# V and U by feature held pair by pair, and float64 weights rounded by one integer addition in pieces of 384 columns

## The chip, the cores and the metric

The kernel runs on one core of one Trainium2 chip. The metric is the device time of one execution in microseconds (us), as the median of the runs shown. A core has five engines that work side by side, each through its own list of instructions in a fixed order: TensorE (PE in the profile, with its weight loads shown as PEld), VectorE (DVE), ScalarE (ACT), GpSimd (POOL) and SyncE (SP), which here does nothing but start transfers. An engine waits when an operand is not ready, and everything behind the waiting instruction on that engine waits with it.

## The reference

A recurrent attention runs over 768 tokens for 4 batches of 8 heads of 40 features (32 pairs of batch and head), and two feed-forward blocks follow on the 3072 tokens of 320 features:

```python
for t in range(S):                                    # S = 768
    y[:, :, t] = einsum('bhd,bhde->bhe', r_t, state)
    Sa = einsum('bhde,bhe->bhd', state, a_t)
    state = state * w_t[:, :, None, :] - einsum('bhd,bhe->bhde', Sa, b_t)
    state = state + einsum('bhd,bhe->bhde', v_t, k_t)
x = y by token                                        # (3072, 320)
x = square(maximum(x @ w_in, 0)) @ w_out              # 320 -> 2048 -> 320
out = ((x @ w_a) * (x @ w_b)) @ w_out2                # 320 -> 1536 -> 320
```

The weight matrices of both blocks are float64 (the inputs are drawn times a float64 scalar), so their 8-byte values reach the chip as pairs of 32-bit words. The kernel makes float32 of them itself.

## The kernel before

**Attention.** The tokens are cut into 24 waves of 32 tokens. Each wave is worked as matrices: `prep1` and `prep2` form products of a, k, b and w alone, every four waves `inv_ops` inverts a triangular matrix in 31 steps on DVE and POOL, and then the wave's own chain runs: `m_z` (PE, then a copy on ACT), `m_s` (copies on ACT), `m_ut` (PE, then the ACT copies at L291 into `VUT`), `m_r` (PE, then ACT copies `VU` and DVE masks `RVR`), `m_st` (PE, then DVE adds the state `VS`) and `m_y` (PE, then DVE scales `Y`, and SP stores it). `VUT` holds V (first 32 of 64 places, loaded by SP at L260) and U (last 32, written by ACT at L291) by feature, for 16 pairs; `m_r` uses the 64 columns of one pair as the weights of a matmul, 32 matmuls a wave, each of which the trace shows as two PE instructions. `prep2` does the same arithmetic with `KBT` in place of `VUT`, and `KBT` is laid out as 16 pairs of 64 columns side by side.

**Weights.** `Weights.load` turns float64 into float32 in pieces: SP loads `raw` (L392), ACT squares the high words (L397), DVE drops tiny values (L398), ACT converts the low words (L401), DVE builds the result and its scale in three instructions (L407, L410, L413), POOL multiplies and adds (L414, L415). For the first block `put` then splits the value into a rounded high part (ACT, L440) and the rest (POOL, L433), and the parts go to DRAM (`w1s`) except for a few blocks of 128 columns of w_in that stay in SBUF (`RESIDENT`). The second block's float32 values go to `w2s`.

**Streams.** From wave 4 on, the first block's matmuls (L430, `Stream`) are put between the matmuls of the waves, at places that `emit` counts out by a rate; blocks that are not resident are loaded from `w1s` again for each of the six groups of 512 tokens (L607), into two buffers. A piece of weights is decoded whenever the matmuls issued add up to a share of `TICK_NS`. After the last wave come the rest of the first block and the whole second block.

**Order.** PE's order is the order of the code from wave 4 on, and a scheduler's before. The other engines' orders come from the same scheduler, and on the chip they are fixed. Every transfer is started by SP, in order.

Of the kernel before, what the change touches and what calls it, by code (L numbers as in the profile page):

```python
# [9 lines left out]
F32 = mybir.dt.float32  # L10
# [7 lines left out]
D = 40  # L18
NP = 16
TW = 32  # L20
GW = 4
TOK = 512

DW = 192
PARTS = ((0, 6), (6, 11), (11, 16))
# [25 lines left out]

LEAST_HIGH = 1.125 * 2.0**-15

# [5 lines left out]
class Attention:  # L59
# [8 lines left out]
    def __init__(s, tc, sb, ps, wakb, rv, vt, xs, n_waves):  # L68
# [3 lines left out]
        def t(name, shape):  # L72
            return sb.tile(shape, F32, name=name)
# [11 lines left out]
        s.Z = t("Z", [128, 320])  # L85
        s.VUT = t("VUT", [104, 64, NP])
        s.VU = t("VU", [128, 640])
# [192 lines left out]
    def m_ut(s, w):  # L280
        inv = s.InvT[:, w % GW]
        for h in range(2):
# [6 lines left out]
            for e in range(2):  # L289
                r = slice(64 * e, 64 * e + D)  # L290
                s.nc.scalar.copy(out=s.VUT[r, 32:64, 8 * h:8 * h + 8].rearrange("p t a -> p a t"), in_=pv[r])  # L291

    def m_r(s, w, part):
# [5 lines left out]
        for p in range(p0, p1):  # L299
            o = slice(80 * (p - p0), 80 * (p - p0) + 80)  # L300
            s.mm(85, ps[64:128, o], s.VUT[0:40, :, p], s.eye_and(s.RVR, slice(0, 40), 0, p))
            s.mm(85, ps[0:64, o], s.VUT[64:104, :, p], s.eye_and(s.RVR, slice(64, 104), 1, p))
        pv = cols(ps[:, 0:80 * n], 80)
# [65 lines left out]
class Weights:  # L369
# [19 lines left out]
    def load(s, src, n, put):  # L389
        nc = s.nc  # L390
        raw = s.sb.tile([128, DW, 2], I32, tag="raw", name="raw", bufs=4)
        nc.sync.dma_start(out=raw[:, 0:n].rearrange("p n k -> p (n k)"), in_=src.bitcast(I32))  # L392

        def first():
            low, high = raw[:, 0:n, 0], raw[:, 0:n, 1].bitcast(F32)
            y = s.sb.tile([128, DW], F32, tag="dy", name="dy", bufs=4)[:, 0:n]
# [5 lines left out]
            return lambda: second(y, low.bitcast(F32))  # L402

        def second(y, low):
            z = s.sb.tile([128, DW], F32, tag="dz", name="dz")[:, 0:n]
            yi, zi = y.bitcast(I32), z.bitcast(I32)
            nc.vector.tensor_scalar(  # L407
                out=zi, in0=yi, scalar1=0x07FFFFFF, scalar2=3, op0=ALU.bitwise_and, op1=ALU.logical_shift_left
            )
            nc.vector.scalar_tensor_tensor(  # L410
                out=yi, in0=yi, scalar=-0x40000000, in1=zi, op0=ALU.bitwise_and, op1=ALU.bitwise_or
            )
            nc.vector.tensor_scalar(out=zi, in0=yi, scalar1=-0x00800000, scalar2=None, op0=ALU.bitwise_and)  # L413
            nc.gpsimd.tensor_tensor(out=low, in0=low, in1=z, op=ALU.mult)  # L414
            s.engine.tensor_tensor(out=y, in0=low, in1=y, op=ALU.add)  # L415
            return lambda: put(y)

        return first


class Moe:
# [13 lines left out]
    def add_w1(s, weights, src, wa, wb, done):  # L435
# [11 lines left out]
        def last(x):  # L447
            put(x, wb[:, 160:320], wb[:, 544:640], wb[:, 320:384])
            done()

        for o in (0, 192):
            weights.add(src[:, o:o + 192], 192, lambda x, o=o: put(x, wa[:, o:o + 192], wa[:, 384 + o:576 + o]))
        weights.add(src[:, 384:544], 160, lambda x: put(x, wb[:, 0:160], wb[:, 384:544]))
        weights.add(src[:, 544:704], 160, last)

# [352 lines left out]
def attention_moe(ctx, tc, wakb, rv, vt, wm1, wm2, nat, out):  # L808
# [367 lines left out]
```

## Time and profile before

| | |
|---|---|
| median of 3 runs | 1364.19 us (1359.73 to 1364.43) |
| profiled execution | 1365.23 us, of which its span 1363.5 us |
| PE busy | 1189.4 us (87% of the span) |
| DVE busy | 836.8 us (61%) |
| ACT busy | 559.5 us (41%) |
| POOL busy | 468.6 us (34%) |

The span is that of one profiled execution, and 1.7 us of its time lie outside it. Shares of busy time are means over stages that differ much, so stretches of the span are read apart: up to about 88 us the first preparations and the first inversion, to 217 us the waves 0 to 3 without a stream, to 890 us the waves 4 to 23 with the stream between them, to 958 us the rest of the first block, and then the second block alone. PEclk is the share of TensorE's full clock that was granted; it has two levels, 1.00 and 0.50 (2.4 and 1.2 GHz), and a figure between them is a mean over both.

### The profile page before, as it was taken

What the parts mean: (1) busy time and instruction counts of PE and PEld (TensorE: products, weight loads), DVE (VectorE), ACT (ScalarE), POOL (GpSimd) and SP (SyncE); (2) the same over time, 40 slices, a digit from 0 to 9 for tenths busy, and PEclk for the clock granted to TensorE, in tenths of its full rate; (3) what the DMA queues carried; (4) which work ended last, traced back from release to release, by engine and by line L of the source; (5) the groups of instructions that cost most, each with busy time, mean ns of one, the idle gap of its engine ahead of it and who ended that gap; (6) DMA issues with size and microseconds to landing.
All of it is one profiled execution on the core that took longest, in us unless ns stands there. A gap on an engine that the chain in (4) does not pass through costs nothing.

```text
span 1363.5 us, 35301 instructions
## 1 busy us (share of the span) xinstructions
PE 1189.4 (87%) x14178; PEld 966.2 (71%) x14178; DVE 836.8 (61%) x1831; ACT 559.5 (41%) x1289; POOL 468.6 (34%) x738
## 2 busy tenths in 40 slices
PE   2536644799889998999899999999998999999997
PEld 2535543676667776777677777778886888888886
DVE  6988898878987898789877733353331332332222
ACT  2224434474455545554554453565221222222221
POOL 3567774755243534453444100000798000000000
PEclk9995555899999999999899999999999999999999
DMA  6225536454366536554563333483221000000000
GB/s 176 52 67 162 157 110 186 124 151 138 109 184 176 160 109 184 161 169 117 172 174 96 106 109 90 160 280 120 75 74 42 12 32 16 20 16 20 14 7 22
DMA packets 87652, 148.28 MB, mean 109 GB/s; under 512 B 11560, under 2 KB 54056, under 8 KB 85416
## 3 DMA queue, kind: packets, MB, share of 16 engines
q1 hardware_dynamic: 87480, 145.94, 36.4%
q8 instruction: 114, 1.87, 0.6%
q14 instruction: 58, 0.48, 0.1%
HBM read 117.06 MB, written 25.69 MB: 105 GB/s over the span
## 4 chain that ended last, share of the span: by engine, by line
PE 46%; POOL 7%; DMA 3%; DVE 3%; issue 1%; ACT 1%; SPq 1%; POOLq 0%; DVEq 0%; ACTq 0%
PE h L430 15%; PE b L430 8%; PE x L430 8%; PE a L104 8%; PE o L430 7%; POOL w_t L683 3%; POOL w_ok L684 3%; DMA raw<-wm 1%; DMA x2s<-xl 1%; DMA w<-w1s 0%; DMA inp<-wakb 0%; DVE tmp L236 0%; DMA xl<-xs 0%; DVE Ball L243 0%; DVE VS L323 0%
## 5 line engine op out<-in xcount | busy, mean ns | idle before, releaser
L430 PE MATMUL h<-xhl,w 128*128 128x512 f32 x768 | 233.7, 425 | 7.0 <-DMA w<-w1s 5.9
L561 DVE TENSOR_TENSOR b<-b,a 128x512 f32<-128x512 f32 x72 | 50.4, 699 | 213.4 <-PE b L430 199.3
L430 PEld LDWEIGHTS h<-xhl,w 128*128 128x128 f32 x768 | 142.2, 196 | 41.2 <-DMA w<-w1s 6.2
L430 PE MATMUL x<-gh,w 128*128 128x512 f32 x480 | 147.7, 420 | 5.0 <-DMA w<-w1s 3.4
L414 POOL TENSOR_TENSOR raw<-raw,dz 128x192 f32<-128x192 f32 (+2 forms) x136 | 82.3, 605 | 164.9 <-DVE dz L413 39.2
L430 PE MATMUL h<-xhl,w2h 128*128 128x512 f32 x360 | 128.0, 396 | 0.0
L104 PEld LDWEIGHTS a<-RVR,VUT 40*64 40x64 f32 x1536 | 96.5, 204 | 41.1 <-issue 20.0
L104 PE MATMUL a<-KA,KBT 40*64 40x80 f32 x1536 | 85.5, 269 | 45.1 <-POOL KBT L182 21.8
L104 PE MATMUL a<-RVR,VUT 40*64 40x80 f32 x1536 | 107.9, 290 | 18.6 <-ACT VUT L291 4.9
L430 PE MATMUL b<-xhl,w2h 128*128 128x512 f32 x360 | 120.9, 401 | 0.0
L104 PEld LDWEIGHTS a<-KA,KBT 40*64 40x64 f32 x1536 | 74.5, 164 | 62.6 <-POOL KBT L182 35.8
L433 DVE TENSOR_TENSOR gl<-h,gh 128x512 fp32r<-128x512 f32 x96 | 66.1, 689 | 84.1 <-ACT h L499 80.4
L563 ACT CAST gh<-b 128x512 fp32r<-128x512 f32 x72 | 42.3, 587 | 163.8 <-DVE b L561 163.8
L430 PEld LDWEIGHTS x<-gh,w 128*128 128x128 f32 x480 | 89.0, 194 | 27.3 <-ACT raw L401 4.1
L497 ACT ACTIVATE h<-h 128x512 f32<-128x512 f32 x96 | 55.9, 582 | 98.5 <-PE h L430 95.6
L430 PE MATMUL x<-gl,w 128*128 128x512 f32 x288 | 95.8, 427 | 0.0
L558 ACT COPY a<-h 128x512 f32<-128x512 f32 x72 | 42.3, 587 | 121.2 <-PE h L430 121.1
L415 POOL TENSOR_TENSOR dy<-raw,dy 128x192 f32<-128x192 f32 (+2 forms) x136 | 88.7, 652 | 8.5
L430 PE MATMUL b<-xhl,w2l 128*128 128x512 f32 x216 | 86.1, 399 | 0.0
L430 PE MATMUL h<-xhl,w2l 128*128 128x512 f32 x216 | 85.9, 397 | 0.0
L430 PE MATMUL o<-w2h,gl 128*128 128x320 f32 x288 | 85.6, 309 | 0.0
L430 PE MATMUL o<-w2l,gh 128*128 128x320 f32 x288 | 85.5, 308 | 0.0
(97 smaller groups left out, 2387.8 us busy)
## 6 DMA issues: line engine op xcount, KB each, us to landing
w<-w1s SPq DMA_DIRECT2D x60, 384.0 KB
w<-w1s SPq DMA_DIRECT2D x60, 320.0 KB
raw<-wm SPq DMA_DIRECT2D x92, 192.0 KB
inp<-wakb SPq DMA_DIRECT2D x48, 322.7 KB
w2f<-w2s SPq DMA_DIRECT2D x12, 544.0 KB
w2s<-dy SPq DMA_DIRECT2D x60, 96.0 KB
raw<-wm SPq DMA_DIRECT2D x32, 160.0 KB
VS<-vt SPq DMA_DIRECT2D x48, 80.0 KB
```

What stands on the lines that cost most here:

```text
L104: s.nc.tensor.matmul(out, lhsT=lhsT, rhs=rhs, start=True, stop=True)
L414: nc.gpsimd.tensor_tensor(out=low, in0=low, in1=z, op=ALU.mult)
L415: s.engine.tensor_tensor(out=y, in0=low, in1=y, op=ALU.add)
L430: s.nc.tensor.matmul(out, lhsT=lhsT, rhs=rhs, start=start, stop=stop)
L433: (engine or s.nc.vector).tensor_tensor(out=out, in0=x, in1=hi.bitcast(F32), op=ALU.subtract)
L497: s.nc.scalar.activation(out=ps, in_=ps, func=ACTF.Relu)
L558: s.nc.scalar.copy(out=a, in_=pa)
L561: s.nc.vector.tensor_tensor(out=pb, in0=pb, in1=a, op=ALU.mult)
L563: s.nc.scalar.copy(out=ch, in_=pb)
L683: nc.gpsimd.tensor_scalar(out=t, in0=x, scalar1=lim, scalar2=None, op0=op)
L684: nc.gpsimd.tensor_tensor(out=s.ok, in0=s.ok, in1=t, op=ALU.mult)
```

## The change

`VUT` becomes `[104, 16, 64]`: a pair's 64 columns lie side by side, as they do in `KBT`. The host no longer exchanges tokens and pairs in v, so that SP's load of V goes to 16 places of 32 tokens (128 bytes) in each row, where it was one run of 512 tokens (2 KB).

A piece of weights has up to 384 columns instead of 192, so that there are 68 pieces instead of 136. In each, DVE takes the sign, ACT converts the low word to a float between 2 and 4 (whose bits count from the exponent's lowest place), ACT takes the absolute value of the high word, DVE raises it to a least value, DVE shifts it left by three bits and puts the sign in, and one 32-bit integer addition on POOL adds the low word's bits, which rounds: two instructions on ACT, three on DVE and one on POOL, where there were two, four and two. `raw` and `dy` have three buffers instead of four, five blocks stay resident instead of six, and the prologue has two `KBT` buffers instead of three.

```diff
-DW = 192
+DW = 384
-PIECES = 8
+PIECES = 4
-DECODE = {0: 28, 1: 28, 2: 28, 3: 28}
-RESIDENT = (2, 4, 7, 9, 12, 14)
+DECODE = {0: 14, 1: 14, 2: 14, 3: 14}
+RESIDENT = (2, 5, 8, 11, 14)
-DEC0 = 6
+DEC0 = 3
...
-        s.VUT = t("VUT", [104, 64, NP])
+        s.VUT = t("VUT", [104, NP, 64])
...
-                out=s.VUT[64 * e:64 * e + D, 0:32], in_=cols(s.rv[w, e, :, 1], NP)
+                out=s.VUT[64 * e:64 * e + D, :, 0:32], in_=cols(s.rv[w, e, :, 1], TW)
...
-                s.nc.scalar.copy(out=s.VUT[r, 32:64, 8 * h:8 * h + 8].rearrange("p t a -> p a t"), in_=pv[r])
+                s.nc.scalar.copy(out=s.VUT[r, 8 * h:8 * h + 8, 32:64], in_=pv[r])
...
-            s.mm(85, ps[64:128, o], s.VUT[0:40, :, p], s.eye_and(s.RVR, slice(0, 40), 0, p))
+            s.mm(85, ps[64:128, o], s.VUT[0:40, p], s.eye_and(s.RVR, slice(0, 40), 0, p))
...
-        raw = s.sb.tile([128, DW, 2], I32, tag="raw", name="raw", bufs=4)
+        raw = s.sb.tile([128, DW, 2], I32, tag="raw", name="raw", bufs=3)
...
-            s.pin(nc.scalar.activation(out=y, in_=high, func=ACTF.Square))
-            s.pin(nc.vector.scalar_tensor_tensor(
-                out=y, in0=y, scalar=LEAST_HIGH**2, in1=high, op0=ALU.is_ge, op1=ALU.mult
...
-            s.pin(nc.scalar.activation(out=low.bitcast(F32), in_=low.bitcast(U32), func=ACTF.Copy, scale=2.0**-52))
...
+            s.pin(nc.vector.tensor_scalar(out=yi, in0=high, scalar1=-0x80000000, scalar2=None, op0=ALU.bitwise_and))
+            s.pin(nc.scalar.activation(
+                out=low.bitcast(F32), in_=low.bitcast(U32), func=ACTF.Copy, bias=2.0, scale=2.0**-51
...
+            s.pin(nc.scalar.activation(out=size, in_=high.bitcast(F32), func=ACTF.Abs))
...
+            nc.vector.tensor_scalar(out=size, in0=size, scalar1=TINY_HIGH, scalar2=None, op0=ALU.max)
+            nc.vector.scalar_tensor_tensor(
+                out=yi, in0=size.bitcast(I32), scalar=3, in1=yi, op0=ALU.logical_shift_left, op1=ALU.bitwise_xor
             )
...
-            nc.vector.tensor_scalar(out=zi, in0=yi, scalar1=-0x00800000, scalar2=None, op0=ALU.bitwise_and)
-            nc.gpsimd.tensor_tensor(out=low, in0=low, in1=z, op=ALU.mult)
-            s.engine.tensor_tensor(out=y, in0=low, in1=y, op=ALU.add)
+            nc.gpsimd.tensor_tensor(out=yi, in0=yi, in1=low, op=ALU.add)
...
-        kbts = [at.KBT] + [pre.tile([104, NP, 64], F32, name=f"KBT{i}") for i in range(1, 3)]
+        kbts = [at.KBT] + [pre.tile([104, NP, 64], F32, name=f"KBT{i}") for i in range(1, 2)]
```

PE's 3026 rows stand in the same order in both programs. On the other engines the scheduler's order moves with the pieces. Counted on ACT, 37 of 136 pieces are begun ahead of wave 4's copy of `Z` before, and 25 of 68 now; ahead of wave 10's it is 88 and 41. Of the 16 blocks, the ten that move need the first 40 pieces before, and the eleven that move need the first 22 now.

On DVE, in wave 1, the rows from the first mask of `RVR` to its last were these before the change:

```order
L307 TENSOR_TENSOR RVR<-a,mask 64x192 x2
L407 TENSOR_SCALAR dz<-dy 128x192
L410 SCALAR_TENSOR_TENSOR dy<-dy,dz 128x192
L413 TENSOR_SCALAR dz<-dy 128x192
L398 SCALAR_TENSOR_TENSOR dy<-dy,raw 128x192
L307 TENSOR_TENSOR RVR<-a,mask 64x160 x2
L407 TENSOR_SCALAR dz<-dy 128x192
L410 SCALAR_TENSOR_TENSOR dy<-dy,dz 128x192
L413 TENSOR_SCALAR dz<-dy 128x192
L307 TENSOR_TENSOR RVR<-a,mask 64x160 x2
```

On DVE, at the same place, they are these now (line numbers are one higher, and L412, L413 and L402 are the new decode):

```order
L308 TENSOR_TENSOR RVR<-a,mask 64x192 x2
L308 TENSOR_TENSOR RVR<-a,mask 64x160 x2
L412 TENSOR_SCALAR dz<-dz 128x320
L413 SCALAR_TENSOR_TENSOR dy<-dz,dy 128x320
L402 TENSOR_SCALAR dy<-raw 128x384
L308 TENSOR_TENSOR RVR<-a,mask 64x160 x2
```

Seven instructions on 192 columns between the masks have become three on 320 or 384.

On SP, where the stream's first weights are fetched back, the rows from the load of wave 4's tokens to the first loads of `w` were these before (`w1s` with its block's number is the stored weights, `xhl` and `xl` the tokens of the first group):

```order
L460 DMA xhl<-xs_57 128x2x512
L462 DMA xl<-xs_57 64x512 x2
L392 DMA raw<-wm 128x320
L257 DMA VS_147<-vt 32x640
L860 DMA w1s_640_87<-w_1750 128x640
L257 DMA VS_147<-vt 32x640
L392 DMA raw<-wm 128x384
L607 DMA w_2148<-w1s_768_70 128x768
L392 DMA raw<-wm 128x384
L860 DMA w1s_768_88<-w_1878 128x768
L607 DMA w_2152<-w1s_768_72 128x768
```

On SP, the rows up to that load of tokens are these now, and the first load of `w` stands two rows ahead of them:

```order
L859 DMA w1s_768_90<-w_1734 128x768
L261 DMA VUT<-rv 40x16x32 x2
L606 DMA w_2048<-w1s_640_71 128x640
L606 DMA w_2050<-w1s_768_72 128x768
L393 DMA raw<-wm 128x640
L859 DMA w1s_640_91<-w_1735 128x640
L393 DMA raw<-wm 128x768
L606 DMA w_2052<-w1s_640_73 128x640
L267 DMA RVR<-rv 40x512 x2
L364 DMA xs_57<-Y 40x4x128 x2
L393 DMA raw<-wm 128x640
L459 DMA xhl<-xs_57 128x2x512
```

The loads of `w` have moved from behind the load of tokens to ahead of it, by about half a wave.

## Rows read from the trace of the kernel before

**Rows 1.** The page's busy times by engine: us, share of the span, instructions.

```profile
PE 1189.4 (87%) x14178; PEld 966.2 (71%) x14178; DVE 836.8 (61%) x1831; ACT 559.5 (41%) x1289; POOL 468.6 (34%) x738
```

**Rows 2.** Windows: stretch, length, PE, PEld, DVE, ACT, POOL busy, PEclk, DMA share, GB/s.

```profile
88.00:217.00 129.00, 76.96 (x1724) 69.64 (x1720) 116.31 (x289) 57.72 (x175) 91.39 (x167) 0.57 0.49 148
217.00:240.00 23.00, 13.66 (x67) 9.89 (x64) 18.49 (x34) 8.75 (x22) 11.97 (x17) 0.61 0.62 185
240.00:400.00 160.00, 142.95 (x2277) 109.28 (x2276) 136.39 (x331) 86.83 (x228) 86.12 (x149) 0.93 0.48 136
400.00:760.00 360.00, 339.10 (x5455) 259.47 (x5453) 296.46 (x706) 188.92 (x453) 149.13 (x264) 0.97 0.53 151
760.00:890.00 130.00, 129.42 (x1953) 99.98 (x1952) 54.99 (x109) 62.13 (x121) 2.58 (x2) 1.00 0.41 128
890.00:1363.00 473.00, 457.50 (x2269) 390.27 (x2267) 141.81 (x204) 137.20 (x237) 85.56 (x65) 0.99 0.16 51
```

**Rows 3.** Waits of PE, 88 to 217 us: total us, times, longest us.

```profile
PE a L104 <- DVE RVR L307: 10.0, 9, 3.5
...
PE a L104 <- DVE ini L153: 6.7, 1, 6.7
```

**Rows 4.** Waits of PE, 217 to 240 us.

```profile
PE h L430 <- DMA w<-w1s: 5.9, 2, 5.1
PE x L430 <- DMA w<-w1s: 3.4, 1, 3.4
```

**Rows 5.** Tile views of KBT and VUT, weight loads: ns min/median/max, first and last start.

```profile
L104 PEld LDWEIGHTS a<-KA,KBT x1536: 129/133/228, 15.0 to 731.7; 40*64 40x64 f32 x192
...
L104 PEld LDWEIGHTS a<-RVR,VUT x1536: 181/201/228, 89.7 to 867.3; 40*64 40x64 f32 x192
```

**Rows 6.** Timeline of PE: start, us for the run, instruction, count, idle before.

```profile
121.89 1.60 PE L104 MATMUL a<-RVR,VUT 40*64 40x80 f32 x20 [2.01 <-DVE dz L413]
123.76 1.60 PE L104 MATMUL a<-KA,KBT 40*64 40x80 f32 x20 [0.27 <-ACT dy L397]
...
514.89 1.56 PE L104 MATMUL a<-RVR,VUT 40*64 40x80 f32 x22
...
699.68 2.00 PE L104 MATMUL a<-RVR,VUT 40*64 40x80 f32 x32
...
728.99 1.32 PE L104 MATMUL a<-KA,KBT 40*64 40x80 f32 x32
```

**Rows 7.** Windows of DVE's instructions on tile dy: stretch, length, busy, PEclk, DMA share.

```profile
88.00:217.00 129.00, 56.91 (x150) 0.57 0.49 148
240.00:400.00 160.00, 50.74 (x135) 0.93 0.48 136
400.00:760.00 360.00, 84.31 (x239) 0.97 0.53 151
```

**Rows 8.** Groups by form on DVE: busy us, mean ns of one, idle before.

```profile
L410 DVE SCALAR_TENSOR_TENSOR dy<-dy,dz 128x192 int32<-128x192 int32 x92 | 42.8, 466 | 2.4
...
L413 DVE TENSOR_SCALAR dz<-dy 128x192 int32<-128x192 int32 x92 | 27.0, 294 | 2.2
...
L410 DVE SCALAR_TENSOR_TENSOR dy<-dy,dz 128x128 int32<-128x128 int32 x12 | 4.8, 402 | 0.3
```

**Rows 9.** Groups by form and by line on POOL.

```profile
L415 POOL TENSOR_TENSOR dy<-raw,dy 128x192 f32<-128x192 f32 x92 | 62.1, 674 | 6.2
...
L684 POOL TENSOR_TENSOR w_ok<-w_ok,w_t 128x480 f32<-128x480 f32 x32 | 39.1, 1223 | 2.7
```

**Rows 10.** Groups by form on ACT, copies out of PSUM.

```profile
L291 ACT COPY VUT<-a 40x256 f32<-40x256 f32 x96 | 57.1, 594 | 28.4 <-PE a L104 26.9
L206 ACT COPY KBS<-a 64x240 f32<-64x240 f32 x48 | 17.0, 354 | 20.1 <-PE a L104 19.3
```

**Rows 11.** Timeline of SP: the load of V for the next wave.

```profile
490.79 0.71 SPq L260 DMA_DIRECT2D VUT<-rv  x2
```

**Rows 12.** Timeline of ACT in the prologue: the first piece of weights.

```profile
25.37 0.37 ACT L397 ACTIVATE dy<-raw 128x192 f32<-128x192 f32 x1 [7.65 <-DMA raw<-wm]
```

More of the change, by code (lines that the diff above doesn't have):

```diff
@@ L50 @@
 NL = 6
-LEAST_HIGH = 1.125 * 2.0**-15
+TINY_HIGH = 2.0**-15
 def cols(ap, n):
@@ L300, in m_r @@
             o = slice(80 * (p - p0), 80 * (p - p0) + 80)
-            s.mm(85, ps[64:128, o], s.VUT[0:40, :, p], s.eye_and(s.RVR, slice(0, 40), 0, p))
-            s.mm(85, ps[0:64, o], s.VUT[64:104, :, p], s.eye_and(s.RVR, slice(64, 104), 1, p))
+            s.mm(85, ps[64:128, o], s.VUT[0:40, p], s.eye_and(s.RVR, slice(0, 40), 0, p))
+            s.mm(85, ps[0:64, o], s.VUT[64:104, p], s.eye_and(s.RVR, slice(64, 104), 1, p))
         pv = cols(ps[:, 0:80 * n], 80)
@@ L390, in load @@
         nc = s.nc
-        raw = s.sb.tile([128, DW, 2], I32, tag="raw", name="raw", bufs=4)
+        raw = s.sb.tile([128, DW, 2], I32, tag="raw", name="raw", bufs=3)
         nc.sync.dma_start(out=raw[:, 0:n].rearrange("p n k -> p (n k)"), in_=src.bitcast(I32))
         def first():
-            low, high = raw[:, 0:n, 0], raw[:, 0:n, 1].bitcast(F32)
-            y = s.sb.tile([128, DW], F32, tag="dy", name="dy", bufs=4)[:, 0:n]
-            s.pin(nc.scalar.activation(out=y, in_=high, func=ACTF.Square))
-            s.pin(nc.vector.scalar_tensor_tensor(
-                out=y, in0=y, scalar=LEAST_HIGH**2, in1=high, op0=ALU.is_ge, op1=ALU.mult
-            ))
-            s.pin(nc.scalar.activation(out=low.bitcast(F32), in_=low.bitcast(U32), func=ACTF.Copy, scale=2.0**-52))
-            return lambda: second(y, low.bitcast(F32))
@@ L404, in second @@
[L404 to L408, printed above, removed]
-            )
-            nc.vector.scalar_tensor_tensor(
-                out=yi, in0=yi, scalar=-0x40000000, in1=zi, op0=ALU.bitwise_and, op1=ALU.bitwise_or
-            )
-            nc.vector.tensor_scalar(out=zi, in0=yi, scalar1=-0x00800000, scalar2=None, op0=ALU.bitwise_and)
-            nc.gpsimd.tensor_tensor(out=low, in0=low, in1=z, op=ALU.mult)
-            s.engine.tensor_tensor(out=y, in0=low, in1=y, op=ALU.add)
+            low, high = raw[:, 0:n, 0], raw[:, 0:n, 1]
@@ new lines, in first @@
+            y = s.sb.tile([128, DW], F32, tag="dy", name="dy", bufs=3)[:, 0:n]
+            yi = y.bitcast(I32)
+            s.pin(nc.vector.tensor_scalar(out=yi, in0=high, scalar1=-0x80000000, scalar2=None, op0=ALU.bitwise_and))
+            s.pin(nc.scalar.activation(
+                out=low.bitcast(F32), in_=low.bitcast(U32), func=ACTF.Copy, bias=2.0, scale=2.0**-51
+            ))
+            size = s.sb.tile([128, DW], F32, tag="dz", name="dz")[:, 0:n]
+            s.pin(nc.scalar.activation(out=size, in_=high.bitcast(F32), func=ACTF.Abs))
@@ L416, in second @@
+            return lambda: second(y, low, size)
+        def second(y, low, size):
+            yi = y.bitcast(I32)
+            nc.vector.tensor_scalar(out=size, in0=size, scalar1=TINY_HIGH, scalar2=None, op0=ALU.max)
+            nc.vector.scalar_tensor_tensor(
+                out=yi, in0=size.bitcast(I32), scalar=3, in1=yi, op0=ALU.logical_shift_left, op1=ALU.bitwise_xor
+            )
+            nc.gpsimd.tensor_tensor(out=yi, in0=yi, in1=low, op=ALU.add)
             return lambda: put(y)
@@ L447, in last @@
         def last(x):
-            put(x, wb[:, 160:320], wb[:, 544:640], wb[:, 320:384])
+            put(x, wb[:, 0:320], wb[:, 384:640], wb[:, 320:384])
             done()
[L451 to L454, printed above, removed]
+        weights.add(src[:, 0:384], 384, lambda x: put(x, wa[:, 0:384], wa[:, 384:768]))
+        weights.add(src[:, 384:704], 320, last)
     def load_x(s, h, src):
@@ L949, in attention_moe @@
             for w in range(GW):
-                at.prep1(w + 1, kbts[(w + 1) % 3], inps[(w + 1) % GW])
+                at.prep1(w + 1, kbts[(w + 1) % 2], inps[(w + 1) % GW])
                 if w == 0:
@@ L953, in attention_moe @@
                 for i in range(len(PARTS)):
-                    at.prep2(w, kbts[w % 3], i)
+                    at.prep2(w, kbts[w % 2], i)
                 at.gather(w)
-            at.prep1(GW + 1, kbts[2], inps[1])
+            at.prep1(GW + 1, kbts[1], inps[1])
             steps, inv_end = at.inv_ops(0)
@@ L972, in attention_moe @@
             for i in range(len(PARTS)):
-                at.prep2(w, kbts[w % 3], i)
+                at.prep2(w, kbts[w % 2], i)
             at.gather(w)
```

3 lines of the change are left out of this document (1 added, 2 removed).

## The prediction

> **What bounds the kernel now.** I read the busy times of the page first, then windows by stage, and then who waited for whom inside the stages. TensorE is busy for 87% of the span [rows 1], but the stages differ. From 890 us on PE is busy for 457.5 of 473 us at a granted clock of 0.99, and no edit reaches that stage, so about 473 us stay as they are. From 240 to 890 us PE is busy for 94% (611.5 of 650 us) at 0.93 to 1.00 of the clock: here PE's own work is the bound, with 38 us of idle time before 760 us. From 88 to 217 us, in waves 0 to 3, PE is busy for only 77 of 129 us while DVE is busy for 116 (90%), and the clock stands at 0.57, mostly its lower level of 1.2 GHz [rows 2]. Most of PE's idle time there ends on DVE (10.0 us on the masks of `RVR`, 6.7 us on the last part of an inversion) [rows 3]. Between 217 and 240 us the stream of the first block starts late, because its weights have not come back from DRAM: 5.9 and 3.4 us [rows 4].
>
> **A, the weight loads of `m_r`.** With `VUT` a weight load takes 201 ns (median), with `KBT` 133 ns, though both load 64 columns on 40 partitions [rows 5]; what differs is that the columns stand 64 bytes apart in `VUT` and side by side in `KBT`. At the upper clock 32 instructions of `m_r` take 2.00 us (62.5 ns each) and 32 of `prep2` take 1.32 us (41.3 ns each) with the same 80 columns streamed; at the lower clock 20 of either take 1.60 us [rows 6]. The change gives `VUT` the layout of `KBT`, so I take 21.2 ns off each of 64 instructions in each of 20 waves at the upper clock: 27.1 us, times the 94% of the stage in which PE works, 25 us. In waves 0 to 3 this gives nothing. The ends are 0 and 27 us.
>
> The Trainium skill, page "TensorE: Matmul & The Clock Gate", section "LDWEIGHTS (loading the stationary operand)", makes the time of a weight load a matter of the column count alone; by that rule term A would be 0 and the sum 25 us higher. The two medians of [rows 5] at one column count speak against it, so the row decides.
>
> **B, waves 0 to 3.** DVE's decode takes 56.9 us of the stretch from 88 to 217 us, in 150 instructions, or 37.5 pieces at 1.52 us [rows 7]. In the new order 24 pieces stand between the first `Z` copies of waves 0 and 4. The new three instructions on 384 columns are not in the trace. At the least they take as long as three on 192 (294, 294 and 466 ns, 1.05 us), at the most twice that (2.1 us); from 128 to 192 columns the two-input form goes from 402 to 466 ns, 1 ns a column [rows 8], and by that slope they take 486, 486 and 658 ns. I take 1.6 us, since a fixed part shows in the rows. DVE then spends 24 x 1.6 = 38 us, 18 less (7 to 32 less). POOL is relieved too: the integer addition lies between one addition on 192 columns (0.67 us) and two (1.35 us), and a two-input operation on 480 columns takes 1.22 us [rows 9], so about 1.0 us for what took two operations on each of two pieces. The copies into `VUT` drop from 594 ns to what a copy without gaps takes, 354 ns for 240 columns [rows 10], so some 370 ns, four a wave on the chain between `m_ut` and `m_r`: 3.6 us in four waves. In later waves the stream's matmuls cover them; without that cover they would be 18 us. Since the remaining waits of PE are partly those of a chain with ACT in it, I take 14 us for all of B, from ends of 0 and 32.
>
> **C, the start of the stream.** The order has the first loads of `w` ahead of the load of tokens now, about half a wave earlier, since the pieces that the moving blocks need are begun before wave 4 (22 needed, 25 begun; before 40 and 37). Half a wave is 16 us (129 / 4 / 2), more than the waits of 5.9 and 3.4 us [rows 4]. I take 8 of the 9.3 us; at the least nothing.
>
> **D, idle time of PE from 240 to 760 us.** It is 17.0 us before 400 us and 20.9 us after [rows 2]. DVE's decode there is 50.7 and 84.3 us [rows 7], and DVE is busy for 85 and 82% of these stretches. In waves 4 to 9 there stand 16 pieces instead of 51 (26 instead of 77 us of DVE), later 27 instead of 48 (43 instead of 72 us). I take half of the first and 6 us of the second: 15 us. The ends are 0 and 38: the chain of a wave keeps its latencies, and PE comes round to them 1.3 us sooner in each wave.
>
> **E, the clock.** A grant of 0.93 over 160 us and of 0.97 over 360 us costs 11.2 + 10.8 = 22 us of work at full speed [rows 2]. If the first stretch comes to the grant of the second, 6.4 us return; I take 7, between 0 and 22.
>
> **F, what is added.** One more block is fetched for each of six groups (704 KB each, 4.2 MB), while DMA is busy for about half of the stage [rows 2]; two buffers and the matmuls between hide it, and if not, 4.2 MB at 150 GB/s are 28 us, the far end. V's load becomes 640 runs of 128 bytes for each half instead of 40 of 2 KB. It is started at 490.8 us [rows 11] and `m_r` of the next wave begins at 514.9 us [rows 6], so it has 24 us, and the wait of SP behind it is for issue alone. The first piece of weights is twice as long: in the prologue ACT already waits 7.65 us for it, with copies for DVE behind [rows 12], and 192 KB more at the stage's pace are 1 to 2 us. The second `KBT` buffer less makes POOL wait for a `prep2` two waves back; DVE's scans come between, so I count nothing (a whole `prep2` at the lower clock would be 64 x 80 ns = 5 us a wave [rows 6]). DVE now takes the sign straight from `raw`, so that a late piece holds DVE's masks and adds where it held ACT first; with half as many pieces I count nothing more. For F I take 5 us, from 0 to 30.
>
> The page "DMA: Bandwidth & Descriptors" of the Trainium skill, section "Specifications", asks for at least 512 bytes a transfer for line rate and says that shorter ones are read, modified and written. No row shows a run of 128 bytes; by that rule the load of V takes longer than its share of bytes, and what it delays is the wait for V in the third rival below.
>
> **Sum.** 25 + 14 + 8 + 15 + 7 - 5 = 64 us less than the profiled execution's 1365.2 us, which stands 1 us above the median of the runs: 1301 us.
>
> **Rivals.**
> 1. The waits stay. PE's waits in the waves are those of chains through ACT and DVE, not of a crowded DVE, so B, D and E give nothing: 1365 - 25 - 8 + 5 = 1337 us. For it: idle time remains at 94% busy. Against it: DVE at 90% and pieces between the masks. Chance 0.16.
> 2. Waves 0 to 3 return to the upper clock. PE's 77 us there shrink by up to half; with DVE's relief B becomes about 35 us: 1280 us. Against it: PE has to become denser first, and a faster PE waits more. Chance 0.10.
> 3. The weight loads stay at 201 ns, or V's short runs land late by as much as A gives (1.3 us a wave beyond the 24 us): A is 0, 1326 us. Chance 0.07.
> 4. Slower: the integer addition on POOL is slow. Without its decode (37.5 pieces at some 1.3 us, 48 us) POOL has 43 us of other work in the 129 us [rows 2, 9], 11 of 32 us a wave. At seven pieces a wave, POOL sets the pace above (32 - 11) / 7 = 3 us for one addition; at 4.8 us the 50 us of the other gains are used up, and at 6 us the time is 1365 - 50 + 4 x 7 x 3 = 1399 us. Against it stands the 1.22 us of [rows 9], though that is not an integer operation. Chance 0.04.
> 5. The orders of the scheduler set one wait for another, and nothing changes beyond 0.5%: about 1365 us. Chance 0.03.
>
> **How the numbers follow.** The forecast of 1301 us, with 1280 to 1322 as its own range, gets 0.60. The range from 1272 to 1338 us reaches to rivals 1, 2 and 3 and leaves out rivals 4 and 5 and the tails. A difference of 0.5% (7 us) is about what these runs can tell from none, as they spread over 5 us. Faster by more: 0.60 + 0.16 + 0.10 + 0.07 = 0.93; within: 0.03; slower: 0.04.
>
> **What would show it.** A: weight loads of `VUT` near 133 ns, and 32 instructions of `m_r` in about 1.3 us. B: wave 4 begins near 200 us, with DVE's new three instructions at 1.3 to 1.9 us a piece. C: no wait for `w` at the stream's start. D and E: 15 us less idle time and a grant near 0.97 from 240 to 400 us. F: no waits for `VUT` or `w`. The prediction fails if POOL's addition takes over 3 us, if PE waits as long as before although DVE is free, or if ACT and DVE stand behind late pieces of `raw`.

## The result, and the profile after

The changed kernel takes 1324.28 us (median of 4 runs, 1322.66 to 1325.55) where the kernel before takes 1363.55 us beside it: a ratio of 0.9717 (95% interval 0.9694 to 0.9739), 39 us less where the prediction had 64 us less. Its profiled execution takes 1325.22 us with a span of 1323.5 us.

The page's busy times of the changed kernel, by engine, against [rows 1]:

```profile
PE 1151.0 (87%) x14178; PEld 934.9 (71%) x14178; DVE 743.3 (56%) x1491; ACT 518.9 (39%) x1121; POOL 359.3 (27%) x502
```

DVE has lost 94 us of work, POOL 109 and PE 38. To see where the 40 us of the span went, I cut both traces where ACT starts the copies of `Z`, one a wave. Windows of the kernel before, for waves 0 to 3, wave 4, and waves 5 to 22 (columns as in [rows 2]):

```profile
69.02:205.61 136.59, 73.80 (x1630) 66.74 (x1632) 122.51 (x304) 52.32 (x161) 99.46 (x196) 0.63 0.41 124
205.61:272.85 67.24, 42.28 (x550) 32.63 (x547) 58.95 (x137) 30.85 (x88) 39.93 (x62) 0.71 0.54 158
272.85:851.63 578.78, 548.01 (x8914) 419.01 (x8915) 444.54 (x1052) 299.58 (x711) 214.60 (x380) 0.97 0.49 141
```

The same windows of the changed kernel:

```profile
70.55:205.11 134.56, 67.90 (x1604) 63.56 (x1606) 109.92 (x232) 51.79 (x128) 82.75 (x140) 0.67 0.55 168
205.11:266.81 61.70, 40.33 (x572) 32.35 (x571) 41.71 (x88) 22.82 (x55) 18.27 (x23) 0.67 0.41 111
266.81:813.90 547.09, 518.53 (x8914) 392.31 (x8915) 379.72 (x831) 268.75 (x611) 144.13 (x238) 0.97 0.54 152
```

| stretch | before | after | difference |
|---|---|---|---|
| up to the first copy of `Z` | 69.0 | 70.5 | +1.5 |
| waves 0 to 3 | 136.6 | 134.6 | -2.0 |
| wave 4 | 67.2 | 61.7 | -5.5 |
| waves 5 to 22 | 578.8 | 547.1 | -31.7 |
| wave 23 and all that follows | 511.9 | 509.6 | -2.3 |
| span | 1363.5 | 1323.5 | -40.0 |

Two things are to be seen. In waves 0 to 3 DVE has 12.6 us less to do and the stretch is only 2.0 us shorter, so that DVE stands idle for 24.6 us in place of 14.1. In waves 5 to 22 PE has 29.5 us less to do, while its idle time, 30.8 us before, is still 28.6 us.

The weight loads of `VUT` in the changed kernel (tile view, ns min/median/max), and one run of `m_r` on PE's timeline; they answer to [rows 5] and [rows 6]:

```profile
L105 PEld LDWEIGHTS a<-RVR,VUT x1536: 128/133/229, 91.2 to 828.3; 40*64 40x64 f32 x192
```

```profile
668.23 1.32 PE L105 MATMUL a<-RVR,VUT 40*64 40x80 f32 x32
```

A load takes 133 ns instead of 201, and 32 instructions take 1.32 us instead of 2.00, the time of `prep2`. The new decode on DVE, POOL's addition and the copies into `VUT`, in groups by form (busy us, mean ns of one):

```profile
L413 DVE SCALAR_TENSOR_TENSOR dy<-dz,dy 128x384 int32<-128x384 int32 x40 | 24.6, 614 | 1.1
L402 DVE TENSOR_SCALAR dy<-raw 128x384 int32<-128x384 int32 x40 | 17.4, 435 | 7.4 <-DMA w2s<-dy 3.5 <-POOL w L434 2.0 <-DMA raw<-wm 1.9
L412 DVE TENSOR_SCALAR dz<-dz 128x384 f32<-128x384 f32 x40 | 16.4, 410 | 21.1 <-ACT dz L407 20.8
```

```profile
L416 POOL TENSOR_TENSOR dy<-dy,raw 128x384 int32<-128x384 int32 x40 | 42.2, 1054 | 154.0 <-DVE dy L413 92.3 <-DMA VUT<-rv 15.9 <-issue 15.3
```

```profile
L292 ACT COPY VUT<-a 40x256 f32<-40x256 f32 x96 | 35.2, 367 | 13.5 <-PE a L105 11.9
```

A piece of 384 columns costs DVE 1.46 us and POOL 1.05 us in the mean over the whole kernel. In waves 0 to 3 DVE's three instructions take 11.6, 12.7 and 17.4 us (L402, L412, L413), some 41 us for the 25 pieces there, so 1.6 us each. What stopped DVE in waves 0 to 3 of the changed kernel (waits: us in all, times, longest):

```profile
DVE dy L402 <- DMA raw<-wm: 8.3, 3, 4.2
DVE BH L228 <- issue: 4.8, 1, 4.8
DVE dy L402 <- POOL w L434: 4.1, 2, 2.0
```

In the same stretch of the kernel before, DVE waited most for POOL's multiplication, never longer than 1.7 us, and the inversion's start (`BH`) cost almost nothing:

```profile
DVE dz L407 <- POOL raw L414: 5.3, 8, 1.7
DVE BH L227 <- DMA Ball<-KA: 0.2, 1, 0.2
```

L402 is the instruction that takes the sign. One such place on DVE's timeline (start, us, instruction, idle before it):

```profile
124.99 0.33 DVE L402 TENSOR_SCALAR dy<-raw 128x320 int32<-128x320 int32 x1 [2.12 <-DMA raw<-wm]
125.33 1.41 DVE L308 TENSOR_TENSOR RVR<-a,mask 64x192 f32<-64x192 f32 x4
```

The masks of `RVR`, for which PE waits, are next in DVE's order and cannot pass. PE's waits from 88 to 220 us, which answer to [rows 3]:

```profile
PE a L105 <- DVE RVR L308: 16.0, 6, 5.9
PE a L105 <- DVE ini L154: 10.9, 1, 10.9
PE a L105 <- DVE Y L361: 9.4, 4, 3.5
```

At the stream's start, from 217 to 240 us, no wait for `w` is left of the 9.3 us in [rows 4]: SP's first load of `w` starts at 188.2 us, before it was 213.0 us. In their place PE waits longer for the inverse (the wait on `ini` L154, the DVE instruction just behind the inversion, 10.9 us instead of 6.7), and for the preparation that follows:

```profile
PE a L105 <- DVE ini L156: 6.6, 1, 6.6
```

Windows of the old stretches, for the clock of [rows 2]:

```profile
240.00:400.00 160.00, 147.17 (x2512) 112.21 (x2511) 113.30 (x244) 76.33 (x178) 50.82 (x76) 0.93 0.50 139
400.00:760.00 360.00, 341.57 (x5741) 258.31 (x5735) 267.53 (x593) 181.35 (x414) 105.16 (x175) 0.97 0.58 163
```

The grants are 0.93 and 0.97, as before. PE's idle time in these stretches is 31.3 us, where [rows 2] have 38.0.

### The profile page after: what moved, and what is told of

It is laid out like the page before. It is cut to its first block, busy times and chain, and to the rows that moved or that the text cites. A ratio compares the mean times of both kernels' runs of the same rounds, so it can differ in the third digit from the quotient of the medians.

```text
span 1323.5 us, 33997 instructions
## 1 busy us (share of the span) xinstructions
PE 1151.0 (87%) x14178; PEld 934.9 (71%) x14178; DVE 743.3 (56%) x1491; ACT 518.9 (39%) x1121; POOL 359.3 (27%) x502
## 4 chain that ended last, share of the span: by engine, by line
PE 54%; DVE 16%; POOL 7%; DMA 5%; issue 3%; ACT 1%; SPq 0%; DVEq 0%; POOLq 0%; ACTq 0%
PE h L431 18%; PE a L105 10%; PE x L431 10%; PE b L431 8%; PE o L431 7%; POOL w_t L682 3%; DVE tmp L237 3%; DVE Ball L244 3%; POOL w_ok L683 3%; DMA inp<-wakb 2%; DVE RVR L308 1%; DVE VS L324 1%; DVE Y L361 1%; DVE gl L434 1%; DMA Ball<-KA 1%
## 5 line engine op out<-in xcount | busy, mean ns | idle before, releaser
L431 PE MATMUL h<-xhl,w 128*128 128x512 f32 x768 | 230.3, 420 | 2.5 <-DVE xhl L434 2.4
L560 DVE TENSOR_TENSOR b<-b,a 128x512 f32<-128x512 f32 x72 | 50.3, 699 | 213.0 <-PE b L431 199.5
L416 POOL TENSOR_TENSOR dy<-dy,raw 128x384 int32<-128x384 int32 (+1 forms) x68 | 68.0, 1000 | 207.3 <-DVE dy L413 125.9
L105 PEld LDWEIGHTS a<-RVR,VUT 40*64 40x64 f32 x1536 | 68.7, 152 | 27.9 <-issue 15.1
L105 PE MATMUL a<-RVR,VUT 40*64 40x80 f32 x1536 | 79.7, 256 | 8.0 <-ACT VU L305 2.4
L431 PEld LDWEIGHTS b<-xhl,w2h 128*128 128x128 f32 x360 | 68.3, 191 | 15.9
```

Source lines behind the costliest of these rows:

```text
L105: s.nc.tensor.matmul(out, lhsT=lhsT, rhs=rhs, start=True, stop=True)
L416: nc.gpsimd.tensor_tensor(out=yi, in0=yi, in1=low, op=ALU.add)
L431: s.nc.tensor.matmul(out, lhsT=lhsT, rhs=rhs, start=start, stop=stop)
L560: s.nc.vector.tensor_tensor(out=pb, in0=pb, in1=a, op=ALU.mult)
```

## The experiments

25 us of the forecast gain are missing: 12 in waves 0 to 3 (term B), and most of the rest in waves 5 to 22, where A, D and E together had more than the 31.7 us found. For waves 0 to 3 the theories were that these waves are a chain of latencies and decode is not what they wait for, or that DVE's relief is real and something in the change takes it back: the length of the instructions, the buffers, or the amount of decode. For waves 5 to 22 they were that the layout gives its price and the decode little, or that the two meet in the same waits. Twelve kernels ran, each beside the kernel before. Stretches of each are cut as above, from one execution each, and a stretch can differ by some us without a cause that is known here: in five kernels with the same 25 pieces of the new arithmetic and three buffers (the changed kernel, decode alone, room made, sign later and POOL's halves) waves 0 to 3 last from 130.2 to 134.6 us.

**The layout alone.** The kernel before with the lines of the change on `VUT` and v:

```diff
-        s.VUT = t("VUT", [104, 64, NP])
+        s.VUT = t("VUT", [104, NP, 64])
...
-            s.mm(85, ps[64:128, o], s.VUT[0:40, :, p], s.eye_and(s.RVR, slice(0, 40), 0, p))
+            s.mm(85, ps[64:128, o], s.VUT[0:40, p], s.eye_and(s.RVR, slice(0, 40), 0, p))
```

> The kernel before with V and U held pair by pair, and nothing else of the change; the order of all instructions stays as it was. Theory 1 (the layout is worth what term A and the shorter copies say, and the rest of the change only some 13 us): 26 us for the m_r matmuls in waves 4 to 23 and some 3 us for the copies in waves 0 to 3, so 1333 to 1339 us, with weight loads of VUT at 133 ns. Theory 2 (much of the gain in the later waves comes from a freer DVE, and the layout gives less than its price because PE then waits for what it no longer covers): above 1345 us.

1352.69 us, ratio 0.9925 (0.9906 to 0.9944), 9 to 10 us less: theory 2. Waves 5 to 22 of this kernel:

```profile
275.84:845.96 570.12, 531.49 (x8914) 399.51 (x8915) 443.23 (x1052) 282.82 (x710) 215.14 (x380) 0.96 0.51 144
```

The weight loads take 133 ns here too. By the price of term A, 1.36 us a wave, 18 waves should lose 24.4 us; PE's work falls by 16.5 us, with the grant at 0.96 instead of 0.97 (0.01 of 570 us is 6 us of the rest), and its idle time rises from 30.8 to 38.6 us. Waves 0 to 3 last 136.6 us as before, so the shorter copies into `VUT` gave nothing there. The profile is of an execution of 1358.35 us, 5.7 us above the median, so the stretch may be some us too long.

**The decode alone.** The changed kernel with those lines the other way round, as in the kernel before:

```diff
-        s.VUT = t("VUT", [104, NP, 64])
+        s.VUT = t("VUT", [104, 64, NP])
```

> The changed kernel with VUT in the old layout: all of the new decode, its pieces and buffers. Theory 1: the changed kernel's 1324 us plus the layout's 26 to 29 us, 1350 to 1354 us, with most of the 10 to 14 us below the kernel before at the stream's start in wave 4. Theory 2: 1340 us or less, since the decode would then give 20 us and more by itself.

1340.12 us, ratio 0.9835 (0.9805 to 0.9866), some 21 us less, at the edge of theory 2. Waves 5 to 22:

```profile
264.97:829.50 564.53, 549.63 (x8914) 421.78 (x8915) 380.56 (x831) 285.90 (x611) 144.12 (x238) 0.96 0.50 147
```

PE works as long as before (549.6 us), and its idle time is halved, from 30.8 to 14.9 us. That is what term D counted, 15 us. With the layout on top, PE works 31.1 us less and waits 13.7 us more: 28.6 us in the changed kernel. A faster PE uses up the slack that a freer DVE had made. In time the two edits do not take from each other, though: these waves are 8.7 us shorter by the layout alone, 14.3 by the decode alone and 31.7 by both.

One place where the layout's saved work comes back is the wait for the masks of `RVR`, which DVE makes out of what `m_r` has computed. In waves 5 to 22 it is this for the kernel before, the layout alone and the changed kernel, and it is not among PE's waits with the decode alone:

```profile
PE a L104 <- DVE RVR L307: 2.1, 2, 1.9
PE a L104 <- DVE RVR L307: 5.9, 5, 2.4
PE a L105 <- DVE RVR L308: 9.0, 7, 3.0
```

**The new arithmetic in pieces of 192, and the old one in pieces of 384.** Both have the new layout. The first is the kernel before in all else, buffers, constants and resident blocks too:

```diff
-            s.pin(nc.scalar.activation(out=y, in_=high, func=ACTF.Square))
...
+            s.pin(nc.scalar.activation(out=size, in_=high.bitcast(F32), func=ACTF.Abs))
...
-            s.engine.tensor_tensor(out=y, in0=low, in1=y, op=ALU.add)
+            nc.gpsimd.tensor_tensor(out=yi, in0=yi, in1=low, op=ALU.add)
```

> The kernel before with the new layout and the new arithmetic, but still in pieces of 192 columns, with four buffers of raw and dy, six resident blocks and three KBT buffers. Theory 1 (waves 0 to 3 are a chain of latencies, and DVE's decode is not what they wait for): as the changed kernel, 1320 to 1330 us. Theory 2 (the relief of DVE is real, but long instructions on 384 columns take it back, by holding up the masks, the inversion and the transfers): waves 0 to 3 become some 10 us shorter than in the changed kernel, so 1305 to 1318 us.

1342.91 us, ratio 0.9847 (0.9823 to 0.9872): outside both. The second is the changed kernel with the old arithmetic, the same lines the other way round:

```diff
-            nc.gpsimd.tensor_tensor(out=yi, in0=yi, in1=low, op=ALU.add)
+            nc.gpsimd.tensor_tensor(out=low, in0=low, in1=z, op=ALU.mult)
+            s.engine.tensor_tensor(out=y, in0=low, in1=y, op=ALU.add)
```

> The changed kernel with the old arithmetic (four instructions on DVE, two on POOL) on pieces of 384 columns. If the length of the pieces is what takes the relief back, this is clearly slower than the layout alone (1333 to 1339 us): 1340 us or more, since DVE's and POOL's instructions are long and are many as well. If the count of instructions on DVE is what matters, it lies between the layout alone and the changed kernel, 1326 to 1335 us. By theory 1, where neither matters to waves 0 to 3, it stands within 5 us of the changed kernel, as the stream starts as early.

1344.73 us, ratio 0.9872 (0.9849 to 0.9896): above the 1340 us that the expectation gave to long pieces, but not slower than the layout alone, which itself turned out slower than that expectation took it. It lies between the layout alone and the changed kernel, as the count of instructions would have it. Waves 0 to 3 of either, the first and then the second:

```profile
68.95:211.44 142.49, 72.42 (x1616) 66.19 (x1618) 122.54 (x317) 66.41 (x211) 99.12 (x193) 0.76 0.52 156
```

```profile
69.14:210.74 141.60, 69.66 (x1604) 64.09 (x1606) 128.32 (x246) 50.81 (x127) 106.99 (x148) 0.63 0.51 157
```

Both are longer there than the changed kernel's 134.6 us, so the length of the pieces is not what takes the relief back. Their DVE is busy for 122.5 and 128.3 us instead of 109.9. The orders show why the first is no better than the old arithmetic: 53 pieces of 192 are begun ahead of wave 4, where the kernel before begins 37. That pointed to the amount of decode in these waves. In columns, the changed kernel's 25 wide pieces are about a third more than those 37, too (pieces have 384 or 320 columns, and 192 or 160).

**Without the decode's arithmetic.**

```diff
-            s.pin(nc.scalar.activation(out=size, in_=high.bitcast(F32), func=ACTF.Abs))
-            return lambda: second(y, low, size)
+            s.pin(nc.scalar.activation(out=y, in_=high.bitcast(F32), func=ACTF.Copy))
+            return lambda: lambda: put(y)
```

> The changed kernel without the arithmetic of the decode: the pieces are still fetched, ACT copies the high words into dy, and DVE's three instructions, POOL's integer addition and two of ACT's are left out, so the weights and the output are wrong. Theory 1 (waves 0 to 3 are a chain of latencies through PE, ACT, DVE and the serial inversion, and decode is not what they wait for): from the first Z copy to the fifth still 125 us or more instead of 134.6, and 1305 us or more in all. Theory 2 (DVE's remaining 41 us of decode there still set the pace): the four waves shrink by 20 us or more, to 115 us or less, and the whole to 1300 us or less.

1294.33 us, ratio 0.948 (0.9431 to 0.9529). Waves 0 to 3:

```profile
71.45:184.87 113.42, 60.96 (x1604) 57.97 (x1606) 74.40 (x172) 50.94 (x127) 57.21 (x118) 0.70 0.63 196
```

21 us shorter: decode sets the pace there, and theory 1 (a chain of latencies) falls. The same 25 pieces come in by DMA, at 196 GB/s, so it is not the transfers either. Still, 113 us remain where DVE has only 74 us of work.

**Fewer pieces in waves 0 to 3.** The number of pieces to a tick, 10 instead of 14:

```diff
-DECODE = {0: 14, 1: 14, 2: 14, 3: 14}
+DECODE = {0: 10, 1: 10, 2: 10, 3: 10}
```

> The changed kernel with DECODE at 10 pieces instead of 14 in waves 0 to 3, so that some 18 instead of 25 pieces are begun ahead of wave 4, about as many columns as in the kernel before (37 pieces of half the width). The first loads of w move back behind the load of tokens. If the larger amount of decode in waves 0 to 3 is what took B back: these waves fall from 134.6 to 125 us or less, and the stream's late start costs some 8 us again, 1320 to 1326 us in all. If decode does not matter to waves 0 to 3: they stay above 131 us, and the kernel takes 1328 to 1336 us.

1316.72 us, ratio 0.9653 (0.9607 to 0.9699). Waves 0 to 3 and wave 4, and PE's wait there:

```profile
69.97:186.47 116.50, 66.44 (x1604) 62.64 (x1606) 101.03 (x214) 41.60 (x106) 71.09 (x126) 0.77 0.47 144
186.47:258.16 71.69, 37.63 (x572) 29.57 (x571) 53.61 (x102) 31.39 (x72) 32.34 (x32) 0.66 0.54 171
```

```profile
PE h L431 <- DMA w<-w1s: 22.9, 2, 19.6
```

With 18 pieces, about the columns of the kernel before, waves 0 to 3 take 116.5 us: 18 us less than the changed kernel, 20 less than the kernel before, and 3 more than without decode. Ten of the 18 us go again in wave 4, since PE waits 22.9 us for `w`. That wait is also what term C had named, seen from the other side.

The same line with 12:

```diff
-DECODE = {0: 14, 1: 14, 2: 14, 3: 14}
+DECODE = {0: 12, 1: 12, 2: 12, 3: 12}
```

> The changed kernel with DECODE at 12 pieces in waves 0 to 3, so that 22 pieces, just what the moving blocks need, are begun ahead of wave 4. If the cost of a piece there is even, waves 0 to 3 lie halfway, near 125 us, the loads of w come some 10 us earlier against the stream's start than at pace 10, and the kernel takes 1312 to 1318 us. If the cost comes as a step, when the pieces no longer fit between the masks, waves 0 to 3 stay at 131 us or more and it takes 1320 to 1326 us.

1330.72 us, ratio 0.9772 (0.9718 to 0.9827). Waves 0 to 3 take 128.7 us:

```profile
70.70:199.42 128.72, 66.39 (x1604) 62.25 (x1606) 106.53 (x224) 47.49 (x118) 79.06 (x136) 0.67 0.48 150
```

So 18, 22 and 25 pieces give 116.5, 128.7 and 134.6 us: 3.1 and 2.0 us for each further piece, more than the 1.6 us that one takes of DVE there. With the spread of the kernels with 25 pieces the second figure lies between 0.5 and 2.0 us; over all seven it is 2.0 to 2.6 us a piece. The total is worse than either theory had it; waves 5 to 22 are 10.7 us longer than in the changed kernel, 2.5 of them PE's work. Why, I did not find out.

**The sign later.** The sign instruction moved from the first of the decode's steps to the second:

```diff
-            s.pin(nc.vector.tensor_scalar(out=yi, in0=high, scalar1=-0x80000000, scalar2=None, op0=ALU.bitwise_and))
...
         def second(y, low, high, size):
+            nc.vector.tensor_scalar(out=yi, in0=high, scalar1=-0x80000000, scalar2=None, op0=ALU.bitwise_and)
```

> The changed kernel, but DVE takes the sign in the later of the two steps, with the other two instructions, when the piece has long landed and its dy buffer is free. In the changed kernel DVE stood idle for 8 us in waves 1 to 3 at that instruction, for the landing of raw and for POOL's split of an earlier piece, with the masks of RVR behind it. If that wait is what took B back: PE's 16 us of waiting for RVR fall by half, and the kernel takes 1314 to 1320 us. If the inversion and the chain set the end of wave 3 anyway: within 4 us of the changed kernel, 1320 to 1328 us.

1362.31 us, ratio 0.9983 (0.9961 to 1.0005): the whole gain is lost. The experiment did not do what it was meant to. Without its fixed place in the program's order the scheduler moved the instruction up, in 38 of 68 cases by one or two pieces, and from 340 to 760 us DVE now waits for the store that empties the `dy` buffer:

```profile
DVE dy L410 <- DMA w2s<-dy: 67.0, 20, 6.4
```

In the changed kernel that wait is 3.5 us for all pieces of 384 columns (the group of L402 above). It shows how dear a wait for a buffer is in DVE's order, and it says nothing on waves 0 to 3, where DVE still waits 11.5 us at the sign instruction.

**A fourth buffer.** As no room was left, two kernels with room made the same way are compared: the first two changes are in both, the two of `bufs` in one.

```diff
-RESIDENT = (2, 5, 8, 11, 14)
+RESIDENT = (2, 6, 10, 14)
-        kbts = [at.KBT] + [pre.tile([104, NP, 64], F32, name=f"KBT{i}") for i in range(1, 2)]
+        kbts = [at.KBT] + [pre.tile([104, NP, 64], F32, name=f"KBT{i}") for i in range(1, 1)]
...
-        raw = s.sb.tile([128, DW, 2], I32, tag="raw", name="raw", bufs=3)
+        raw = s.sb.tile([128, DW, 2], I32, tag="raw", name="raw", bufs=4)
...
-            y = s.sb.tile([128, DW], F32, tag="dy", name="dy", bufs=3)[:, 0:n]
+            y = s.sb.tile([128, DW], F32, tag="dy", name="dy", bufs=4)[:, 0:n]
```

> The changed kernel with four buffers for raw and dy instead of three; to make room, four resident blocks instead of five and a single KBT buffer in the prologue. Only waves 0 to 3 are compared, with the run beside it that has the same room made and three buffers. If DVE's waits at the sign instruction (4.0 us for the landing of raw, 4.1 us for POOL's split out of dy) are what took B back, waves 0 to 3 shrink by 5 us or more and these waits go. If it is the amount of decode, they stay within 3 us, and DVE waits somewhere else.

> The changed kernel with four resident blocks and a single KBT buffer in the prologue, and three buffers of raw and dy as in the changed kernel: what the run with four buffers is compared with. Waves 0 to 3 as in the changed kernel, 132 to 137 us, by either theory; the prologue and the stream are a few us longer, since POOL waits for prep2 and one more block moves.

With a single KBT buffer, `prep2` of each of the waves 0 to 4 reads what `prep1` of the next wave has written, so both kernels compute something else, with the same instructions. With four buffers 1336.77 us (ratio 0.9807, 0.976 to 0.9853), with three 1346.97 us (0.9881, 0.9837 to 0.9926). Waves 0 to 3 with four buffers and then with three:

```profile
90.43:213.25 122.82, 67.13 (x1604) 63.01 (x1606) 112.24 (x231) 51.42 (x127) 81.79 (x134) 0.66 0.57 182
```

```profile
89.43:219.81 130.38, 68.31 (x1604) 63.92 (x1606) 109.02 (x231) 51.91 (x127) 81.08 (x134) 0.77 0.54 171
```

And DVE's waits in them, with four buffers and then with three:

```profile
DVE BH L228 <- DMA Ball<-KA: 2.3, 1, 2.3
DVE dy L402 <- DMA raw<-wm: 0.6, 1, 0.6
```

```profile
DVE dy L402 <- DMA raw<-wm: 6.3, 3, 2.5
DVE dy L402 <- POOL w L434: 4.1, 2, 2.0
DVE BH L228 <- issue: 3.6, 1, 3.6
```

At the same 25 pieces the fourth buffer takes 7.6 us off these waves and 9.8 us off the wait at the sign instruction. The kernel with three buffers missed its own expectation of 132 to 137 us by 1.6 us, and its first copy of `Z` starts 19 us later than in the changed kernel, so 7.6 us is its worth in this pair; it stands clear of the spread, as all five kernels with 25 pieces and three buffers took 130.2 us or more. `raw` and `dy` got their fourth buffer together, and which of them gives how much is not shown.

**POOL's addition in two halves.**

```diff
-            nc.gpsimd.tensor_tensor(out=yi, in0=yi, in1=low, op=ALU.add)
+            n = y.shape[1] // 2
+            for c in (slice(0, n), slice(n, 2 * n)):
+                nc.gpsimd.tensor_tensor(out=yi[:, c], in0=yi[:, c], in1=low[:, c], op=ALU.add)
```

> The changed kernel with POOL's integer addition in two instructions of half the columns each. If DVE's steps of the inversion are held up by the length of POOL's instruction that runs beside them (11 steps of over 0.7 us in the second inversion, against 5 before), they get shorter, the second inversion loses 2 to 4 us, and the kernel takes 1318 to 1323 us. If it is POOL's total time that holds DVE up, or if nothing waits for it, 1323 to 1332 us, as POOL's work grows by the fixed part of one more instruction a piece.

1325.81 us, ratio 0.9714 (0.9663 to 0.9765): no change from the changed kernel's 0.9717. Waves 0 to 3 take 133.6 us instead of 134.6. The length of POOL's instruction is not what decides. Nor is it POOL's work beside the inversion in all: DVE's instructions on the inversion's `tmp` are busy for 47.7 us from 60 to 230 us in the kernel before and for 48.6 us in the changed kernel.

**A better pace.**

```diff
-DECODE = {0: 14, 1: 14, 2: 14, 3: 14}
+DECODE = {0: 10, 1: 10, 2: 10, 3: 18}
```

> The changed kernel with DECODE at 10 pieces in waves 0 to 2 and 18 in wave 3: some 15 pieces begun ahead of wave 3 and 22 ahead of wave 4. At pace 10 waves 0 to 3 took 116.5 us, but the stream then waited 22.9 us for w; wave 3 lasted 30.3 to 30.9 us at each pace. If the pieces cost little in wave 3, where the serial inversion ends last anyway: waves 0 to 3 at 116 to 122 us, the wait for w at 10 us or less, and 1304 to 1314 us in all. If four more pieces in wave 3 draw out the inversion by what they take elsewhere (2.6 us each): waves 0 to 3 at 125 us or more, and 1316 to 1324 us.

1313.40 us, ratio 0.9629 (0.9602 to 0.9657), the lowest time with all of the decode: some 11 us less than the changed kernel. Its 3 us on pace 10 lie within the two intervals. Waves 0 to 3 and wave 4:

```profile
72.49:192.08 119.59, 66.63 (x1604) 62.75 (x1606) 104.72 (x217) 47.31 (x119) 76.44 (x128) 0.76 0.50 156
192.08:253.26 61.18, 39.22 (x572) 31.03 (x570) 48.23 (x100) 25.54 (x60) 24.02 (x32) 0.70 0.59 170
```

Against pace 10, the four more pieces cost 3.1 us in waves 0 to 3, and wave 4 is 10.5 us shorter, with no wait for `w` among PE's waits. So pieces are cheapest in wave 3; that the serial inversion, which ends last there, is what covers them was only argued.

## Why the prediction was right, and where not

The direction and the main term held, and the time lies in the wide range but 2 us beyond the forecast's own 1280 to 1322 us: between the forecast and rival 1. Waits stayed, as rival 1 had it, though for another reason than the one it named.

**A** was right in its mechanism: 133 ns, 1.32 us for 32 instructions, and nothing at the lower clock. The rule of the Trainium skill (page "TensorE: Matmul & The Clock Gate", section "LDWEIGHTS (loading the stationary operand)") that the column count alone sets a weight load does not hold here, as 64 columns on 40 partitions took 201 ns and now take 133 ns. The step that failed is the one from work to time: the sum took PE's waits as they were and booked 94% of its saved work as saved time. Measured by adding the layout to either decode, it is worth 9 to 10 us with the old one (0.9925) and 16 with the new (1340.12 to 1324.28), not 25. Of the 24.4 us of waves 5 to 22, 7.9 and 13.7 us come back as waits of PE. That the second worth is the larger all the same comes with the grant, which goes from 0.97 to 0.96 in the first pair and from 0.96 to 0.97 in the second, some 6 us of work each way (an estimate, 0.01 of the stretch); whether the edits do that is not shown.

**D** was right for itself: 15.9 us less idle time in the decode-only kernel, 15 forecast. In the changed kernel only 2.2 us of it are left, since the waits that A brings back stand in the same idle time. The prediction saw that PE would come round to the chain 1.3 us sooner in each wave and gave it no price.

**B** failed in the step from DVE's work to the time of the stretch. The price of 1.6 us a piece came true there, and DVE's work fell by 12.6 us (18 forecast), but the stretch by 2.0 us where 14 were forecast. The runs put two things in its place. The change does about a third more of the decode in these waves, and the seven pieces beyond 18 cost 2.0 to 2.6 us each there; with about the old amount of columns they take 116.5 us, which is more than the forecast gain, though wave 4 is then 10 us longer than in the changed kernel. Three buffers in place of four cost 7.6 us at 25 pieces; these two overlap, and their shares can't be told apart. That was named in F, that a late piece would hold DVE's masks "where it held ACT first", and counted at nothing "with half as many pieces". The copies into `VUT` gave nothing, where 3.6 us were counted.

**C** was right: the loads start 24.9 us earlier, and the 9.3 us of waiting are gone (8 forecast). But PE waits 4.2 us more for the inverse of waves 4 to 7, which comes out of waves 0 to 3 later, and 6.6 us more for the next preparation, so that wave 4 is only 5.5 us shorter in all.

**E** gave nothing: the grants are 0.93 and 0.97 in both. **F** held in its other parts: the first copy of `Z` comes 1.5 us later (1 to 2 forecast for the longer first piece), PE waits 0.5 us for `w` in the whole stream, and V's runs of 128 bytes delay nothing that PE waits for. The rule of the Trainium skill (page "DMA: Bandwidth & Descriptors", section "Specifications") that transfers under 512 bytes lose line rate would make these loads longer; no run here shows what they cost by themselves.

Rival 2 did not come: PE works 66 to 68 us in waves 0 to 3 of the changed kernel and of the other paces, at mean grants of 0.67 to 0.77. These means are too high to go by, since up to the first change of the clock that a trace holds they count 1.00. In [rows 2] that is up to 101.6 us. At pace 10 it is up to 125.3 us, and there matmuls of 80 columns still take 80 ns each, the time of the lower level in [rows 6] (window, and a run on PE's timeline):

```profile
70.00:125.30 55.30, 30.20 (x692) 29.10 (x694) 45.00 (x103) 18.95 (x49) 31.34 (x59) 1.00 0.41 124
119.91 1.60 PE L105 MATMUL a<-KA,KBT 40*64 40x80 f32 x20 [0.94 <-DVE RVR L308]
```

Rival 3 fell with A's 133 ns, and rival 4 too: the addition takes 1.05 us, not 3.

## What to carry to other kernels

Work saved on the engine that bounds a stage is not yet time saved: part of it comes back as waits for the other engines of the chain, so run the edit alone, and on top of the other, before its price goes into a sum. An edit that makes a background task cheaper may also make it run earlier or denser; count its work per stretch, not per instruction. An instruction that waits for a buffer belongs on an engine whose order has nothing urgent behind it, or needs one buffer more.

## What the runs showed of the hardware

DVE instructions that read two operands from SBUF get longer beside some of POOL's. In the changed kernel's second inversion eleven of DVE's 62 products and differences take over 0.7 us, and each runs beside an instruction of POOL (nine times one of the decode, twice the state's) and ends 0.05 to 0.27 us after it. Two products of the inversion in the changed kernel, and POOL's split of weights, by time:

```profile
180.97 1.13 POOL L434 TENSOR_TENSOR w<-dy,w 128x384 fp32r<-128x384 f32 x1
181.28 1.07 DVE L237 TENSOR_TENSOR tmp<-BH,Ball 128x220 f32<-128x220 f32 x1
...
182.85 0.46 DVE L237 TENSOR_TENSOR tmp<-BH,Ball 128x231 f32<-128x231 f32 x1
```

The first of DVE's takes 1.07 us and ends 0.25 us after POOL's; the next, on more columns, takes 0.46 us. The Trainium skill (page "SBUF — State Buffer", section "SBUF: two separate sides") says that a DVE instruction with two SBUF inputs and a GpSimd instruction that reads SBUF exclude each other for a whole instruction, and the rows agree in kind.

POOL's 32-bit integer addition takes 1.05 us on 384 columns, less than twice the 0.67 us of a float32 addition on 192 [rows 9]. It ran beside DVE, so some of that may be waiting. And a layout with the columns 64 bytes apart costs a weight load 68 ns of 201 (medians), at the same columns and partitions; at the lower clock 20 instructions take 1.60 us in either layout [rows 6].
